# Rows of a Fourier stage's first batch: loaded from SBUF in four transfers a quad instead of by way of DRAM

## The chip, the cores and the metric

One Trainium2 chip, one core of it. The metric is device time in microseconds (us) of one execution of the whole program. The kernel before has a median of 1192.6 us in 3 runs (1191.81 to 1194.62).

## What is computed

Two batches of 3008 tokens with 256 features go through a Fourier layer and then through two feed-forward layers, all in float32:

```python
X = np.fft.rfft(x, axis=1)                       # x: (2, 3008, 256)
Yr = X.real @ w_r - X.imag @ w_i + b_r
Yi = X.real @ w_i + X.imag @ w_r + b_i
Y = shrink(Yr, 0.01) + 1j * shrink(Yi, 0.01)     # sign(v) * max(|v| - 0.01, 0)
x = np.fft.irfft(Y, n=3008, axis=1).reshape(6016, 256)
h = x @ moe_w_in                                 # 256 -> 2048
x = (h * clip(h + 3, 0, 6) / 6) @ moe_w_out      # 2048 -> 256
g = x @ moe2_w_gate                              # 256 -> 1536
out = (g * sigmoid(g) * (x @ moe2_w_val)) @ moe2_w_out
```

## The kernel before

The Fourier transform of length 3008 = 47 x 64 is done in two stages of matrix products. The first stage (`pre`, L315, products at L328 and L330) gives, for a batch, 96 rows of 32 x 256 numbers: 24 values of g, two parts and two halves of the real tokens, 32 values of j. A row is 8192 numbers, 32 KB. The first batch's rows lie in one SBUF tile, `first`, one row per partition; those of the second batch lie in `second` and in pieces of a ring.

The second stage (`s2`, L390, products at L397) wants these rows in another shape: for each g, the 4 rows that belong to it and the 32 values of j have to lie on 128 partitions with 256 numbers each. It works on a *quad* of four g at a time, six quads a batch, and its operand is the tile `z`, 128 partitions x 4 x 256, 512 KB, in three buffers. Going from 16 rows on 16 partitions to 128 partitions is the work of DMAs, and in the kernel before all of them go through scratch tensors `Bd` in DRAM.

For the first batch the rows of quad Q are the partitions Q, Q + 6, Q + 12 and so on of `first`, 16 in all. Quad 0 is written to `Bd[0]` from POOL's queue in four column pieces while the first stage still runs (L337, released by `sent`). The quads 1 to 5 are written whole by `group` (L351, L353), from SP's queue, each right after the load of the z before it (`load_q`, L380, L386). So z1 is loaded when `Bd[1]` has landed, and so on. The second batch goes through `Bd[6]` (written at L339 and L357) and its z are loaded at L386 also.

The order is written out by hand in `seq`: the second stage of quad p + 1 (`S`) begins with `ahead`, which issues the table `m` (L373) and the tile z of quad p + 2, so a z is asked for about one quad before it is used. Between them stand the products with the layer's weights (`ln`, L428, products at L441 to L446), the first inverse stage (`ia`, L464, products at L471, table `n`, results sent to `Cd` by POOL) and steps of `conv1`, which loads pieces of the feed-forward weights into `st` (L165) and converts them. SP issues nearly all loads, in program order. The tile framework gives the transfers of SP and ACT eight semaphores, DMAHW0 to DMAHW7, in turn; a transfer that takes one waits until the transfer that had it before has landed.

After these stages, some 190 us into the run, come the feed-forward layers, where TensorE works without a break.

Of the kernel before, what the change touches and what calls it, by code (L numbers as in the profile page):

```python
# [9 lines left out]
F32 = mybir.dt.float32  # L10
# [10 lines left out]
SEQ, DIM, NB = 3008, 256, 2  # L21
N1, NG, NJ, K2 = 47, 24, 32, 64
QN, GW = 2 * N1, 4 * NG

QP = 96
NQ = NG // 4
# [59 lines left out]
def fourier_moe_kernel(ctx: ExitStack, tc: tile.TileContext, x, lin, bias, w1, w2, fwd1, inv2, fwd2,  # L86
                       inv1, out):
    nc = tc.nc
# [3 lines left out]

    ps = ctx.enter_context(tc.tile_pool(name="ps", bufs=1, space=PSUM))
    dram = ctx.enter_context(tc.tile_pool(name="scratch", bufs=1, space=DRAM))
    Bd = [dram.tile([16 if n < NQ else GW, NJ * DIM], F32, name=f"Bd{n}") for n in range(NQ + 1)]
    Cd = [dram.tile([GW, NJ * DIM], F32, name=f"Cd{b}") for b in range(NB)]
    Xd = dram.tile([128, 2, TOK], F32, name="Xd")
    Wd = [dram.tile([128, SLOT * 128], F32, name=f"Wd{f}") for f in range(KF2)]
# [213 lines left out]
    first = w1p.tile([128, NT * TC], F32, tag="w1_o", name="first", bufs=1)  # L312
# [33 lines left out]

    REFILL = {1: 6, 3: 7}
    SINCE = {3: 0, 5: 4, 6: 6, 7: 7}
    bd1 = Bd[NQ].rearrange("(q r) c -> r q c", q=NQ)

    def group(Q):  # L351
        if 0 < Q < NQ:
            nc.sync.dma_start(Bd[Q], first[Q:GW:NQ])  # L353

    def write_second(i):
        c = slice(2 * i * TC, 2 * (i + 1) * TC)
# [10 lines left out]
    bview = [t.rearrange("(g w) (j d) -> (w j) g d", w=4, j=NJ) for t in Bd]  # L367
    cview = [[t[48 * q : 48 * q + 48].rearrange("(g c) (j d) -> (c j) g d", c=2, j=NJ) for q in range(2)] for t in Cd]
    m_t, z_t, n_t, X, yp = {}, {}, {}, {}, {}
# [6 lines left out]
    def load_m(b, Q):  # L376
        if (b, Q) not in m_t:
            m_t[b, Q] = table("m", fwd2, Q, f"m{b}_{Q}", 3)

    def load_q(b, Q):  # L380
        if (b, Q) in z_t or Q >= NQ:
            return
        load_m(b, Q)
        z_t[b, Q] = ap_.tile([128, 4, DIM], F32, tag="z", name=f"z{b}_{Q}", bufs=3)
        src = bview[NQ][:, Q * 4 : Q * 4 + 4, :] if b else bview[Q]
        nc.sync.dma_start(z_t[b, Q], src)  # L386
        if b == 0:
            group(Q + 1)

    def s2(b, Q, dh):  # L390

# [93 lines left out]
    def ahead(p):  # L485
        if p < len(ORDER):
            load_q(*ORDER[p])
# [7 lines left out]
    def L(p):  # L495
        return [lambda h=h: ln(*ORDER[p], h) for h in range(2)]

    def A(p):
        return [lambda: ia(*ORDER[p])] if p >= 0 else []

    P = [lambda n=n: pre(n) for n in range(NB * NT)]
    seq = [prepare] + P[:NT] + [lambda: load_q(0, 0)] + P[NT : NT + 2] + [lambda: load_q(0, 1)]
    seq += P[NT + 2 : NT + 5] + S(0) + P[NT + 5 : NT + 6]
    rest = P[NT + 6 :]
    for p in range(len(ORDER)):
        l, a = L(p), A(p - 1)
# [722 lines left out]
```

## Time and profile before

| | us |
|---|---|
| median of 3 runs | 1192.6 (1191.81 to 1194.62) |
| the profiled execution | 1195.22 |
| its span, first to last instruction | 1193.4 |
| TensorE (PE) busy | 1181.4 |
| VectorE (DVE) busy | 917.5 |
| ScalarE (ACT) busy | 775.5 |
| GpSimd (POOL) busy | 58.4 |
| mean granted TensorE clock | 0.999 of 2.4 GHz |

All times in a profile are from the start of the span. PE is the matmul side of TensorE and PEld its weight load, which overlaps it; SPq is SyncE's queue of DMA issues, and what stands behind an issue is the time that SP took to issue it, not that of the transfer. A transfer's own time is given apart, from issue to landing. L386 is line 386 of the kernel before; the code that loads z and the lines behind it stand two to four lines earlier in the changed kernel. A share of the DMA engines is the time that packets took, divided by that of 16 engines; packets of a stretch are counted by their start.

### The profile page before, as it was taken

What the parts mean: (1) busy time and instruction counts of PE and PEld (TensorE: products, weight loads), DVE (VectorE), ACT (ScalarE), POOL (GpSimd) and SP (SyncE); (2) the same over time, 40 slices, a digit from 0 to 9 for tenths busy, and PEclk for the clock granted to TensorE, in tenths of its full rate; (3) what the DMA queues carried; (4) which work ended last, traced back from release to release, by engine and by line L of the source; (5) the groups of instructions that cost most, each with busy time, mean ns of one, the idle gap of its engine ahead of it and who ended that gap; (6) DMA issues with size and microseconds to landing.
All of it is one profiled execution on the core that took longest, in us unless ns stands there. A gap on an engine that the chain in (4) does not pass through costs nothing.

```text
span 1193.4 us, 17934 instructions
## 1 busy us (share of the span) xinstructions
PE 1181.4 (99%) x6576; PEld 979.7 (82%) x6576; DVE 917.5 (77%) x1630; ACT 775.5 (65%) x1431; POOL 58.4 (5%) x91
## 2 busy tenths in 40 slices
PE   9999999999999999999999999999999999999998
PEld 3888887878888888888889888888888888888997
DVE  5678985898999989989888666766766766766665
ACT  3667765677777777777777655655655655655554
POOL 4011004500000000000000000000000000000000
PEclk9999999999999999999999999999999999999999
DMA  8898534964472563553543544644644644644552
GB/s 300 296 286 248 169 90 126 310 214 161 130 242 102 189 224 138 176 182 141 203 163 119 185 159 159 230 159 159 229 159 159 229 159 159 225 159 159 199 193 72
DMA packets 69208, 219.63 MB, mean 184 GB/s; under 512 B 6672, under 2 KB 29200, under 8 KB 57296
## 3 DMA queue, kind: packets, MB, share of 16 engines
q1 hardware_dynamic: 66144, 209.28, 51.2%
q0 software_dynamic: 2688, 9.05, 2.7%
q8 instruction: 51, 0.84, 0.3%
q14 instruction: 37, 0.30, 0.1%
q10 hardware_dynamic: 288, 0.16, 0.0%
HBM read 172.07 MB, written 46.40 MB: 183 GB/s over the span
## 4 chain that ended last, share of the span: by engine, by line
PE 90%; DMA 4%; DVE 3%; ACT 1%; issue 1%; POOL 1%; SPq 0%; DVEq 0%; ACTq 0%; POOLq 0%
PE acc L127 12%; PE acc L129 12%; PE acc L128 11%; PE P L931 8%; PE P L933 8%; PE P L932 8%; PE Tb L931 4%; PE Tb L933 4%; PE Tb L932 4%; PE Q L931 2%; PE Q L933 2%; PE Q L932 2%; PE p L471 2%; PE p L397 2%; DMA z<-Bd 1%; PE p L330 1%
## 5 line engine op out<-in xcount | busy, mean ns | idle before, releaser
L987 ACT COPY hold<-P 128x512 f32<-128x512 f32 (+1 forms) x224 | 128.3, 573 | 74.9 <-PE P L933 74.9
L613 ACT CAST gated<-r 128x512 fp32r<-128x512 f32 (+1 forms) x160 | 98.2, 614 | 58.4 <-DVE r L978 58.3
L132 DVE TENSOR_TENSOR gated<-s,gated 128x512 fp32r<-128x512 f32 (+1 forms) x144 | 97.4, 676 | 49.7 <-ACT gated L1114 49.5
L127 PE MATMUL acc<-gated,w_o 128*128 128x512 f32 (+1 forms) x320 | 124.1, 388 | 0.0
L132 DVE TENSOR_TENSOR gated<-r,gated 128x512 fp32r<-128x512 f32 (+1 forms) x160 | 107.8, 674 | 21.1 <-ACT gated L613 17.2
L982 DVE TENSOR_TENSOR hold<-Q,hold 128x512 f32<-128x512 f32 (+1 forms) x112 | 75.9, 678 | 62.4 <-PE Q L933 52.9
L128 PE MATMUL acc<-gated,w_o 128*128 128x512 f32 (+1 forms) x320 | 123.3, 385 | 0.0
L129 PE MATMUL acc<-gated,w_o 128*128 128x512 f32 (+1 forms) x320 | 123.2, 385 | 0.0
L974 ACT ACTIVATE r<-hold,consts 128x512 f32<-128x512 f32 (+1 forms) x120 | 85.7, 714 | 43.3 <-DVE hold L982 40.2
L129 PE MATMUL acc<-gated,slot 128*128 128x512 f32 (+1 forms) x288 | 111.1, 386 | 0.0
L127 PE MATMUL acc<-gated,slot 128*128 128x512 f32 (+1 forms) x288 | 111.0, 385 | 0.1
L128 PE MATMUL acc<-gated,slot 128*128 128x512 f32 (+1 forms) x288 | 110.9, 385 | 0.0
L982 DVE TENSOR_TENSOR hold<-P,hold 128x512 f32<-128x512 f32 (+1 forms) x112 | 75.8, 677 | 38.9 <-PE P L933 38.9
L1154 ACT ACTIVATE s<-hold 128x512 f32<-128x512 f32 (+1 forms) x72 | 44.8, 623 | 85.6 <-DVE hold L982 85.6
L931 PE MATMUL P<-xo,slot 128*128 128x512 f32 (+1 forms) x240 | 92.5, 385 | 2.8 <-DVE hold L982 2.7
L982 DVE TENSOR_TENSOR hold<-Tb,hold 128x512 f32<-128x512 f32 (+1 forms) x112 | 75.9, 678 | 24.8 <-PE Tb L933 18.2
L978 DVE SCALAR_TENSOR_TENSOR r<-r,hold 128x512 f32<-128x512 f32 (+1 forms) x120 | 81.2, 677 | 14.3 <-ACT r L974 13.2
L932 PE MATMUL P<-xo,slot 128*128 128x512 f32 (+1 forms) x240 | 91.6, 382 | 0.0
L933 PE MATMUL P<-xo,slot 128*128 128x512 f32 (+1 forms) x240 | 91.6, 382 | 0.0
L1114 ACT CAST gated<-s 128x512 fp32r<-128x512 f32 (+1 forms) x144 | 88.1, 612 | 2.2 <-DVE s L1169 2.2
L1159 ACT ACTIVATE s<-hold 128x512 f32<-128x512 f32 (+1 forms) x72 | 45.0, 625 | 50.8 <-DVE hold L982 50.8
L987 ACT COPY hold<-Tb 128x512 f32<-128x512 f32 (+1 forms) x112 | 64.9, 580 | 7.0 <-PE Tb L933 0.4
(190 smaller groups left out, 2869.8 us busy)
## 6 DMA issues: line engine op xcount, KB each, us to landing
slot<-Wd SPq DMA_DIRECT2D x72, 1152.0 KB, 5.1
slot<-Sd SPq DMA_DIRECT2D x40, 896.0 KB, 4.9
st<-in_w SPq DMA_DIRECT2D x68, 256.0 KB, 5.1
Wd<-slot SPq DMA_DIRECT2D x12, 1152.0 KB, 5.2
z<-Bd SPq DMA_DIRECT2D x12, 512.0 KB, 6.8
Cd<-cs POOLq DMA_DIRECT2D x24, 256.0 KB, 5.2
Xd<-x SPq DMA_DIRECT2D x20, 256.0 KB, 3.1
raw<-Xd SPq DMA_DIRECT2D x5, 1024.0 KB, 7.8
```

The lines of the kernel that those rows point to most:

```text
L127: nc.tensor.matmul(o, wl, xh, start=start, stop=False)
L128: nc.tensor.matmul(o, wh, xh, start=False, stop=False)
L129: nc.tensor.matmul(o, wh, xl, start=False, stop=stop)
L132: nc.vector.tensor_tensor(out=o, in0=full, in1=hi.bitcast(F32), op=ALU.subtract)
L613: nc.scalar.copy(hi[:, :n], g[:, :n])
L931: nc.tensor.matmul(o, wl, x[m][:, 0, :n], start=start, stop=False, skip_group_check=not start)
L932: nc.tensor.matmul(o, wh, x[m][:, 1, :n], start=False, stop=False, skip_group_check=not start)
L933: nc.tensor.matmul(o, wh, x[m][:, 0, :n], start=False, stop=True, skip_group_check=not start)
L974: nc.scalar.activation(r[:, :n], x[:, :n], AF.Relu, bias=three)
L982: nc.vector.tensor_tensor(out=h, in0=x[:, :n], in1=c, op=ALU.add)
L987: nc.scalar.copy(c, x[:, :n])
L1114: nc.scalar.copy(hi[:, :nb], t[:, :nb])
```

## The change

`Bd` shrinks to one tensor of 16 rows for quad 0 and one of 96 rows for the second batch. `group` and its five stores are gone. For quads 1 to 5 of the first batch `load_q` issues four transfers instead of one, each of which reads four rows of `first` and writes one of the four parts of z, 128 KB. Quad 0 and the second batch stay as they were.

```diff
-    Bd = [dram.tile([16 if n < NQ else GW, NJ * DIM], F32, name=f"Bd{n}") for n in range(NQ + 1)]
+    Bd = [dram.tile([GW if b else GW // NQ, NJ * DIM], F32, name=f"Bd{b}") for b in range(NB)]
...
-    bd1 = Bd[NQ].rearrange("(q r) c -> r q c", q=NQ)
-
-    def group(Q):
-        if 0 < Q < NQ:
-            nc.sync.dma_start(Bd[Q], first[Q:GW:NQ])
+    bd1 = Bd[1].rearrange("(q r) c -> r q c", q=NQ)
...
         z_t[b, Q] = ap_.tile([128, 4, DIM], F32, tag="z", name=f"z{b}_{Q}", bufs=3)
-        src = bview[NQ][:, Q * 4 : Q * 4 + 4, :] if b else bview[Q]
-        nc.sync.dma_start(z_t[b, Q], src)
-        if b == 0:
-            group(Q + 1)
+        if b or not Q:
+            nc.sync.dma_start(z_t[b, Q], bview[b][:, Q * 4 : Q * 4 + 4, :])
+            return
+        for g in range(4):
+            a = Q + 4 * NQ * g
+            nc.sync.dma_start(z_t[b, Q][:, g], first[a : a + 4 * NQ : NQ].rearrange("w (j d) -> w j d", j=NJ))
```

SP's queue before, from the load of z0 on. A name's number is the quad (`z_1` is z of quad 1) and then that of its buffer; what stands in brackets are the semaphores that the instruction waits for:

```order
L386 DMA z_0_238<-Bd_60 128x4x256 [waits DMASW5_49,DMASW4_49,DMAHW5_49,DMASW3_49,DMASW2_49]
L353 DMA Bd_61<-first 16x8192 [waits DMAHW6_49,DVE_49,Activation_49]
L373 DMA m_1_258<-in_fwd 128x512 [waits DMAHW7_49]
L386 DMA z_1_260<-Bd_61 128x4x256 [waits DMAHW6_49,DMAHW0_49]
L353 DMA Bd_62<-first 16x8192 [waits DMAHW1_49]
L373 DMA n_0_317<-in_inv 128x512 [waits DMAHW2_49]
L373 DMA m_2_346<-in_fwd 128x512 [waits DMAHW3_49]
L386 DMA z_2_348<-Bd_62 128x4x256 [waits DMAHW1_49,DMAHW4_49,DMASW0_49,DVE_49]
L353 DMA Bd_63<-first 16x8192 [waits DMAHW5_49]
```

The same place in the changed kernel:

```order
L382 DMA z_0_233<-Bd_60 128x4x256 [waits DMASW5_49,DMASW4_49,DMAHW5_49,DMASW3_49,DMASW2_49]
L369 DMA m_1_252<-in_fwd 128x512 [waits DMAHW6_49]
L386 DMA z_1_254<-first 128x1x256 [waits DMAHW7_49,DVE_49,Activation_49]
L386 DMA z_1_254<-first 128x1x256 [waits DMAHW0_49]
L386 DMA z_1_254<-first 128x1x256 [waits DMAHW1_49]
L386 DMA z_1_254<-first 128x1x256 [waits DMAHW2_49]
L369 DMA n_0_313<-in_inv 128x512 [waits DMAHW3_49]
L369 DMA m_2_342<-in_fwd 128x512 [waits DMAHW4_49]
L386 DMA z_2_344<-first 128x1x256 [waits DMAHW5_49,DMASW0_49,DVE_49]
L386 DMA z_2_344<-first 128x1x256 [waits DMAHW6_49]
L386 DMA z_2_344<-first 128x1x256 [waits DMAHW7_49]
L386 DMA z_2_344<-first 128x1x256 [waits DMAHW0_49]
```

The stores and the waits for them (DMAHW6 before z1, DMAHW1 before z2) are gone, z has four entries a quad, and the third of z2 (DMAHW7) now follows the landing of the first of z1. The order on the other engines is the same.

## Rows read from the trace of the kernel before

**Rows 1.** The page: part 1, and part 4, the chain by engine.

```profile
PE 1181.4 (99%) x6576; PEld 979.7 (82%) x6576; DVE 917.5 (77%) x1630; ACT 775.5 (65%) x1431; POOL 58.4 (5%) x91
...
PE 90%; DMA 4%; DVE 3%; ACT 1%; issue 1%; POOL 1%; SPq 0%; DVEq 0%; ACTq 0%; POOLq 0%
```

**Rows 2.** TensorE's waits, whole run: us in total, times, longest us.

```profile
PE p L397 <- DMA z<-Bd: 1.8, 1, 1.8
```

**Rows 3.** Timeline of PE: start us, us, instruction; in brackets idle time before it.

```profile
35.56 2.05 PE L397 MATMUL p<-m,z 128*128 128x128 f32 x16
...
63.04 1.95 PE L397 MATMUL p<-m,z 128*128 128x128 f32 x16
64.92 2.00 PE L471 MATMUL p<-yp,n 64*128 64x256 f32 x16
...
73.73 2.62 PE L397 MATMUL p<-m,z 128*128 128x128 f32 x16 [1.84 <-DMA z<-Bd]
76.28 3.02 PE L471 MATMUL p<-yp,n 64*128 64x256 f32 x16
```

**Rows 4.** Chain that ended last, in order of time: start us, us, what.

```profile
30.52 5.00 DMA z<-Bd
...
62.08 11.52 DMA z<-Bd
```

**Rows 5.** Busy time by stretch; behind POOL's: granted clock, DMA share, GB/s.

```profile
73.70:80.00 6.30, 6.27 (x37) 5.30 (x38) 3.11 (x7) 3.27 (x8) 0.00 (x0) 0.73 0.67 209
```

**Rows 6.** Timeline of SP's queue: start us, us of issuing, transfer.

```profile
24.95 0.40 SPq L386 DMA_DIRECT2D z<-Bd  x1
25.46 0.57 SPq L353 DMA_DIRECT2D Bd<-first  x1
...
30.52 0.38 SPq L386 DMA_DIRECT2D z<-Bd  x1
```

**Rows 7.** Waits of SP's queue: us in total, times, longest us.

```profile
SPq L386 <- DMA Bd<-first: 17.6, 5, 7.6
```

**Rows 8.** Transfers issued from 24 to 26 us: count, KB each, us to landing.

```profile
z<-Bd SPq DMA_DIRECT2D x1, 512.0 KB, 4.0
Bd<-first SPq DMA_DIRECT2D x1, 512.0 KB, 5.0
```

**Rows 9.** DMA from 25 to 72 us by queue: packets, MB, share of 16 engines.

```profile
q1 hardware_dynamic: 5597, 10.84, 68.9%
q0 software_dynamic: 771, 2.63, 19.2%
```

**Rows 10.** Instructions on `first`: ns of issuing, min/median/max, first and last start.

```profile
L353 SPq DMA_DIRECT2D Bd<-first x5: 512/689/2194, 25.5 to 51.0; - x5
```

**Rows 11.** Instructions on `z` from 20 to 75 us, the same columns.

```profile
L386 SPq DMA_DIRECT2D z<-Bd x6: 377/380/4103, 25.0 to 62.1; - x6
```

**Rows 12.** DMA packets from 25.7 to 28.7 us, and q1's share.

```profile
DMA packets 542, 1.02 MB, mean 339 GB/s; under 512 B 15, under 2 KB 527, under 8 KB 527
...
q1 hardware_dynamic: 542, 1.02, 102.1%
```

**Rows 13.** The same from 26.2 to 27.8 us, z0's load alone.

```profile
DMA packets 320, 0.33 MB, mean 205 GB/s; under 512 B 0, under 2 KB 320, under 8 KB 320
...
q1 hardware_dynamic: 320, 0.33, 68.9%
```

**Rows 14.** The same from 132.9 to 134.4 us, a z of the second batch.

```profile
DMA packets 339, 0.33 MB, mean 221 GB/s; under 512 B 15, under 2 KB 339, under 8 KB 339
...
q1 hardware_dynamic: 339, 0.33, 63.1%
```

**Rows 15.** The same from 101.3 to 102.1 us, the load of ct.

```profile
DMA packets 16, 0.18 MB, mean 225 GB/s; under 512 B 0, under 2 KB 0, under 8 KB 0
...
q1 hardware_dynamic: 16, 0.18, 127.9%
```

## The prediction

> **What bounds the kernel now.** I read the page first. TensorE is busy for 99% of the span and makes 90% of the chain that ended last, DMA 4% of it [rows 1]. So the change can pay only where TensorE stands still for a z tile, and it costs wherever it makes one later. The list of TensorE's waits has one such entry in the whole run: 1.8 us, once, at L397 for a z read from Bd [rows 2]. The timeline gives the place: the second-stage products of quad 5 start at 73.73 us after 1.84 us of standing still, and those of quad 1 at 35.56, just behind the landing of z1, issued at 30.52 and 5.00 us on its way, with nothing to spare [rows 3, 4]. The stall has a tail. Quad 5's products took 2.62 us where quad 4's took 1.95, and the inverse products behind them 3.02 against 2.00 [rows 3]: in that stretch the granted clock is 0.73, that is, part of it at 1.2 GHz instead of 2.4 [rows 5]. The tail is (2.62 - 1.95) + (3.02 - 2.00) = 1.7 us, so all that waiting for z costs today is 1.84 + 1.7 = 3.5 us.
>
> Then SP's timeline: load z0 at 24.95, store group 1 at 25.46, load z1 only at 30.52 [rows 6]. SP stood 17.6 us in five waits for those stores to land [rows 7]. Undisturbed, z lands 4.0 us after its issue and a store in 5.0 [rows 8]; z5, issued at 62.08, took 11.5 [rows 4]. From 25 to 72 us the 16 DMA engines are 68.9 + 19.2 = 88.1% busy [rows 9]. This stretch has little DMA time to give away.
>
> **The change, part by part.** *Removed:* five stores of 512 KB, SP's 17.6 us of waiting for them and 2.5 MB of reads from DRAM. On SP the five stores (median 689 ns, [rows 10]) and five loads (380 ns, [rows 11]) give way to 20 loads of about 380 ns: 20 x 0.38 = 7.6 us for 5 x (0.69 + 0.38) = 5.4. SP is on no path there and the 17.6 us of waits go, so I cost these 2.2 us at nothing; were that cover gone, each later quad's z would be some 0.5 us later. Behind a blocked z load stand m, n and the piece of w1 that the conversion needs, all used about a quad later. The order also shows that a transfer waits for the one eight places ahead of it: the third part of z2 waits for the first part of z1. SP may still run about a quad ahead, as far as the three z buffers allow.
>
> *Added:* the same 512 KB per quad, in four transfers that each read four rows of `first`. How they spread over the 16 engines decides. In the stretch with z0 and the first store, the packets over 8 KB are 15, with (1.02 - 0.52) MB between them: one is one 32 KB row [rows 12]. So a store of 16 rows is 16 pieces for 16 engines. Every other transfer of the stretch has 16, 64, 96 or 128 rows on each side; none has four (the code tells it), so the trace doesn't show how four are dealt. I take it that a row goes to one engine as it does in the store: four rows, four engines, and, with nothing in the rows that speaks for rotating, the same four for every part. [...]
>
> The destination rows are 1 KB, so each of the four engines moves 4 x 32 = 128 pieces of 1 KB per quad instead of z's 32 pieces and one 32 KB row. Price of a piece: between 26.2 and 27.8 us only z0 moves, 320 pieces at a share of 0.689: 0.689 x 16 x 1.6 / 320 = 55 ns [rows 13]. Low end: 0.631 x 16 x 1.5 / 324 = 47 ns in a calmer stretch (339 packets less 15 of a few bytes, [rows 14]). High end: the ct load into 48 rows, 16 pieces of 11 KB, 1.279 x 16 x 0.8 / 16 = 1.02 us each, 93 ns per KB [rows 15]. I take 55: same piece, same tile, same stretch. Price of a 32 KB row: (1.021 x 16 x 3.0 - 512 x 0.055) / 15 = 1.39 us [rows 12].
>
> *The sum, for one of the four engines, 25 to 72 us:* busy 0.881 x 47 = 41.4 us, idle 5.6. Off: five z's, 5 x 32 x 0.055 = 8.8, and five rows, 6.9. On: 5 x 128 x 0.055 = 35.2. Net +19.5; the idle 5.6 swallows a part, +13.9. The other traffic left, 41.4 - 15.7 = 25.7 us, loses its competitors for DRAM; at 47 for 55 ns it shrinks by 15%, 3.8 us. So z5 lands 10 to 14 us later, I say 12. TensorE waits for it; the tail at 1.2 GHz stays as it is; behind z5, z of the second batch shifts along, and from there TensorE is the bound and gives nothing back. Waits will not all stand at quad 5: z1 is due at 35.5 and four engines need 7 us for it behind z0, so a stall of about 1 us begins there and grows by 2 to 4 per quad.
>
> At 47 ns: 5 x 128 x 0.047 = 30.1, less 15.7, 5.6 and 3.8, gives +5. At 93: 59.5 - 15.7 - 5.6 = +38. The profiled execution is 1195.2 us (span 1193.4); it would become 1207. It stands 2.6 over the median of 1192.6, so on the median: 1192.6 + 12 = **1204.6 us**.
>
> **Rivals.**
> *A, the parts spread over all engines* (or over different fours). Then every engine has 8.8 + 6.9 - 8.8 = 6.9 us less to do, SP issues z earlier by its lost waits, z5 is there before 71.9, and stall and tail go: 1192.6 - 3.5 = 1189.1. For it: nothing in the trace has four rows, so nothing forbids it. Against: a row has been one engine's piece in the store. It decides if the wait at L397 vanishes. Chance 0.19.
> *B, the four engines also get in each other's way in z's rows.* In the ct load pieces cost 93 ns per KB on 48 rows against 55 on 128 [rows 13, 15], so few rows written at once are dearer. Then +20 to +38, 1213 to 1231. Against: z has 128 rows, and four engines ask for less than sixteen. [...] Chance 0.20.
> *C, four engines, but hidden:* SP runs ahead by what it waited before, and the other traffic shrinks by more than 15%, so that z5 is as late as now. The low price with 3 us more relief does it: 1192.6. For it: a 32 KB row, which is 1.39 us, is 43 ns per KB. Chance 0.12.
>
> **How the numbers follow.** The forecast (+4 to +20) has 0.49, A 0.19, B 0.20, C 0.12. About 0.2% (2.4 us) is what a measurement here can tell from no change. Faster is A, 0.19; within is C, 0.12; slower the rest, 0.69. The range reaches down to A with half a microsecond of margin, 1188.5, and up to 1224, which leaves out the upper half of B; with the forecast alone it would be 1197 to 1213.
>
> **What would show it.** Right: TensorE's waits hold an entry at L397 for z read from first, several times, 10 us or more in all; in the first 90 us the mean DMA share falls well under 0.88 while TensorE waits for DMA, the mark of a few loaded engines; the parts land in far more than 4.0 us; Bd<-first shrinks to POOL's four. Only the size wrong: the same picture with another price per piece. Wrong: no wait for z at L397, parts that land in 3 to 4 us, a granted clock of 1.00 around 74 us (A); or a single wait of about 2 us as now (C).

## The result and the profile after

The changed kernel takes 1200.34 us (median of 5 runs, 1198.56 to 1202.31), the kernel before, in runs beside it, 1192.07 (1191.40 to 1194.62). The ratio is 1.0066, 95% interval 1.0055 to 1.0076: slower by 8.3 us, where 12.5 were forecast from 1192.1 (1204.6, range 1188.5 to 1224). The profiled execution took 1199.77 us, its span is 1198.0.

TensorE's waits of the changed kernel, whole run (us in total, times, longest us):

```profile
PE p L395 <- DMA z<-first: 4.3, 5, 2.1
PE P L929 <- DVE hold L980: 2.6, 3, 1.3
```

The one wait for z of [rows 2] has become five, 4.3 us in all. The timeline of PE shows where they are:

```profile
29.85 1.95 PE L395 MATMUL p<-m,z 128*128 128x128 f32 x16
...
35.73 1.95 PE L395 MATMUL p<-m,z 128*128 128x128 f32 x16
...
45.16 1.38 PE L395 MATMUL p<-m,z 128*128 128x128 f32 x10 [0.32 <-DMA z<-first]
...
54.99 1.95 PE L395 MATMUL p<-m,z 128*128 128x128 f32 x16
...
63.68 2.13 PE L395 MATMUL p<-m,z 128*128 128x128 f32 x16
65.74 2.00 PE L469 MATMUL p<-yp,n 64*128 64x256 f32 x16
...
73.23 0.46 PE L395 MATMUL p<-m,z 128*128 128x128 f32 x2 [0.52 <-DMA z<-first]
74.51 0.49 PE L395 MATMUL p<-m,z 128*128 128x128 f32 x2 [0.82 <-DMA z<-first]
77.12 0.80 PE L395 MATMUL p<-m,z 128*128 128x128 f32 x2 [2.12 <-DMA z<-first]
78.48 2.51 PE L395 MATMUL p<-m,z 128*128 128x128 f32 x10 [0.55 <-DMA z<-first]
80.91 2.81 PE L469 MATMUL p<-yp,n 64*128 64x256 f32 x16
```

Quads 1, 3 and 4 find their z there, and quad 2 waits 0.32 us. Quad 5 gets its four parts one by one, the last at 78.48, against 73.73 in [rows 3]: 0.52 + 0.82 + 2.12 + 0.55 = 4.0 us of waiting. The clock follows (busy time of each engine by stretch; behind POOL's: granted clock, DMA share, GB/s):

```profile
63.00:72.00 9.00, 9.00 (x73) 8.21 (x73) 7.11 (x16) 6.49 (x16) 1.28 (x2) 1.00 0.89 256
72.00:84.00 12.00, 7.99 (x40) 6.19 (x39) 5.48 (x12) 4.02 (x11) 0.00 (x0) 0.72 0.82 248
```

A clock of 0.72 over 12 us is 6.7 us at the lower level, which is 0.50 (that is the granted clock from 75.80 to 82.50 us; in the kernel before it is 0.50 from 75.00 to 78.30), and in part of them TensorE stood still. Measured as the prediction measured it, the tail is (0.46 + 0.49 + 0.80 + 2.51 - 1.95) + (2.81 - 2.00) = 3.1 us, where it was 1.7 in the kernel before; a part of it is not the clock but the cutting of sixteen products into four groups, since two products take 0.46 us by themselves.

Two views tell what the DMA engines did. First, the stretch of 29.0 to 31.1 us, in which nothing but parts of z1 moves (packets, then q1's share of 16 engines):

```profile
DMA packets 202, 0.20 MB, mean 97 GB/s; under 512 B 4, under 2 KB 202, under 8 KB 202
...
q1 hardware_dynamic: 202, 0.20, 27.2%
```

0.272 x 16 = 4.4 engines at work and 97 GB/s, with two parts of 128 KB and more in the queue. A piece costs 0.272 x 16 x 2.1 / 198 = 46 ns, where z0's load took 55 [rows 13]. Second, the packets of the whole run, on the page of the kernel before and on that of the changed one:

```profile
DMA packets 69208, 219.63 MB, mean 184 GB/s; under 512 B 6672, under 2 KB 29200, under 8 KB 57296
```

```profile
DMA packets 69048, 217.01 MB, mean 181 GB/s; under 512 B 6592, under 2 KB 29120, under 8 KB 57216
```

Gone are five stores and five loads with 16 + 512 pieces, and the small packets of these transfers, which I take for their completions, one per engine that takes part; under 512 B there are 80 fewer. A load of 128 rows has sixteen of them (e2 below counts 240 more for 15 loads more). At sixteen each the ten transfers had 160, so the 20 new ones post 80, four each; the stretch above, in which one part of z1 ends, holds four. SP's queue is no longer held by the stores of [rows 7], but by the issues of z's parts, most from quad 4 on (start us, us of issuing, transfer; then ns of one issue, min/median/max):

```profile
31.75 4.20 SPq L386 DMA_DIRECT2D z<-first  x4
...
48.69 8.35 SPq L386 DMA_DIRECT2D z<-first  x4
...
63.41 7.86 SPq L386 DMA_DIRECT2D z<-first  x4
...
L386 SPq DMA_DIRECT2D z<-first x20: 538/980/2712, 26.0 to 69.0; - x20
```

One issue takes 0.98 us in the median where the prediction had 0.38.

From 25 to 72 us the DMA engines are 48.0 + 21.2 = 69.2% busy (88.1% in [rows 9]):

```profile
q1 hardware_dynamic: 4944, 7.26, 48.0%
q0 software_dynamic: 804, 2.76, 21.2%
```

The DMA engines do less in all, and yet z5 comes later: that is the mark of a few loaded engines.

### The profile page after: what moved, and what is told of

It is laid out like the page before. It is cut to its first block, busy times and chain, and to the rows that moved or that the text cites. A ratio compares the mean times of both kernels' runs of the same rounds, so it can differ in the third digit from the quotient of the medians.

```text
span 1198.0 us, 17944 instructions
## 1 busy us (share of the span) xinstructions
PE 1182.5 (99%) x6576; PEld 980.6 (82%) x6576; DVE 917.4 (77%) x1630; ACT 776.7 (65%) x1431; POOL 58.5 (5%) x91
## 4 chain that ended last, share of the span: by engine, by line
PE 88%; DVE 5%; DMA 3%; ACT 2%; SPq 1%; issue 1%; POOL 0%; ACTq 0%; DVEq 0%; POOLq 0%
PE acc L127 11%; PE acc L129 11%; PE acc L128 11%; PE P L929 8%; PE P L931 8%; PE P L930 8%; PE Tb L931 4%; PE Tb L929 4%; PE Tb L930 4%; PE Q L931 2%; PE Q L929 2%; PE Q L930 2%; PE p L469 2%; PE p L330 2%; DMA z<-first 2%; PE p L395 2%
```

## The experiments

**Four rows against four parts.** Both kernels keep the way through DRAM, and both load each z in four transfers of 128 KB. In e1 a transfer has four rows, held apart by padding; in e2 it has 128.

```diff
# e1_dram_four_rows, quads 1 to 5 of the first batch; Bd[1] to Bd[5] are 256 numbers wider
-        nc.sync.dma_start(z_t[b, Q], src)
+        for g in range(4):
+            nc.sync.dma_start(z_t[b, Q][:, g], Bd[Q][4 * g : 4 * g + 4].rearrange("w (j d) -> w j d", j=NJ))
# e2_dram_four_parts
+            nc.sync.dma_start(z_t[b, Q][:, g], bview[Q][:, g])
```

> Three theories. T (mine): a transfer whose source has four rows uses four DMA engines, always the same four; they carry 128 pieces of 1 KB per quad and z5 comes late. I: it is the issuing, four transfers a quad instead of one on SP's queue and its eight semaphores. S: it is the source, pieces read out of four partitions of SBUF are slow. This kernel keeps the way through DRAM (stores included) and loads each of z1 to z5 in four transfers of four rows; the rows in DRAM are padded by 1 KB so that the four rows stay a dimension of their own. T: at 47 ns a piece the four engines carry 5 x (128 - 32) x 0.047 = 22.6 us more than in the kernel before, less 5.6 of idle time: z5 10 to 17 us later, 1200 to 1210, and 12 completion packets fewer for each such transfer than a full one has. I: as the changed kernel, about 1200. S: no SBUF source, 1190 to 1194.

> Way through DRAM as before, each of z1 to z5 loaded in four transfers of 128 rows x 1 KB on each side (128 rows each, no dimension of four). T: 16 engines as before, SP has 15 issues more (about 6 us) beside other work: 1190 to 1195. I: about 1200, since the queue and the semaphores are used as in the changed kernel and the stores come on top. S: 1190 to 1195.

Measured: e1 1208.30 us (ratio 1.0126, 1.0099 to 1.0153), e2 1196.59 (1.0031, 1.0010 to 1.0051), before 1193.04. The source is DRAM in both and the number of issues is the same; the rows alone make 11.7 us. The pages count 6672 packets under 512 B in e1, as many as before, and 6912 in e2: the 20 transfers post 80 completions in e1, four each, and 320 in e2, sixteen each. Stretches in which only z's pieces start show the same, 35.2 to 36.1 us of e1 and then 40.2 to 41.4 of e2:

```profile
DMA packets 87, 0.09 MB, mean 98 GB/s; under 512 B 1, under 2 KB 87, under 8 KB 87
...
q1 hardware_dynamic: 87, 0.09, 27.5%
```

```profile
DMA packets 381, 0.35 MB, mean 289 GB/s; under 512 B 42, under 2 KB 381, under 8 KB 381
...
q1 hardware_dynamic: 381, 0.35, 94.6%
```

z's pieces keep 4.4 engines busy and move at 98 GB/s, against 15 engines and 289 GB/s. The other engines are not idle in e1's stretch: a view that begins half a microsecond earlier has twelve packets of over 8 KB, rows of a store that are still under way.

```profile
DMA packets 145, 0.52 MB, mean 375 GB/s; under 512 B 5, under 2 KB 133, under 8 KB 133
```

A piece costs 0.275 x 16 x 0.9 / 86 = 46 ns in e1, as in the changed kernel, though the source here is DRAM. That is T, and it ends S: four rows are slow without an SBUF source, and with one the piece is no dearer. It is not the length of an issue either: in e1 an issue takes 0.53 us in the median, less than in the changed kernel, and the loss is larger. But e2 is not free. Its 1196.59 us lie above T's 1190 to 1195, 3.5 us over the kernel before; four transfers a quad in place of one cost something of their own, and no run shows by which way.

**Another queue, and one row at a time.** e3 issues the 20 transfers from POOL, e4 cuts each into four of one row, whose 32 pieces T deals to 16 engines, which nothing had shown before this run.

```diff
# e3_direct_pool
-            nc.sync.dma_start(z_t[b, Q][:, g], first[a : a + 4 * NQ : NQ].rearrange("w (j d) -> w j d", j=NJ))
+            nc.gpsimd.dma_start(z_t[b, Q][:, g], first[a : a + 4 * NQ : NQ].rearrange("w (j d) -> w j d", j=NJ))
# e4_direct_one_row
+            for w in range(4):
+                r = a + NQ * w
+                nc.sync.dma_start(z_t[b, Q][32 * w : 32 * w + 32, g], first[r : r + 1].rearrange("w (j d) -> w j d", j=NJ))
```

> The changed kernel with the 20 four-row transfers issued from POOL's queue instead of SP's. [...] I: SP has 20 issues fewer, 1188 to 1193. S: source unchanged, about 1200 or more.

> The changed kernel with each four-row transfer cut into four of one row (32 pieces of 1 KB to 32 partitions, the slowest dimension that is not 1 is 32 on both sides), 16 a quad on SP's queue. T: such a transfer is dealt to 16 engines, two pieces each, so the load is even; SP issues 80 transfers of about 0.4 us, 6.4 us a quad of some 8.5, and eight in flight of 32 KB: 1189 to 1196. I: four times the issues of the changed kernel, 1205 to 1220. S: 1200 or more.

e3: 1202.02 us (1.0077, 1.0058 to 1.0097). I (1188 to 1193) missed; S (about 1200 or more) hit, and had been ruled out by e1. T had left two outcomes open: parts spread over all 16 engines, 1188 to 1193, which missed, and the same four engines as on SP's queue, 1199 or more, which hit. Yet the parts do not all use the same four engines here: between 24 and 26 us, when only POOL's queue moves, its share is 42.4%, 6.8 engines. Nor is z5 sent late: POOL issues it from 63.22 us on, SP in the changed kernel from 63.41. But it stands right behind two stores of Cd and one of the second batch in POOL's queue, and the DMA share from 63 to 72 us is 0.95. Issued from 60 to 72 us are (count, KB each, us to landing):

```profile
Bd<-second SPq DMA_DIRECT2D x1, 768.0 KB, 13.6
st<-in_w SPq DMA_DIRECT2D x2, 256.0 KB, 10.1
z<-first POOLq DMA_DIRECT2D x4, 128.0 KB, 15.7
```

These transfers take 10.1 to 15.7 us to land, and TensorE stands still for 5.44 us before quad 5. Whether the queue or the traffic made z5 late is not settled, so e3 decides nothing about T beyond those 6.8 engines.

e4: 1224.89 us (1.0276, 1.0253 to 1.0299). T had 1189 to 1196 and fell short by 29 us; I, with 1205 to 1220, by 5. T took 0.4 us for an issue. SP's queue shows the sixteen of quads 1 and 3:

```profile
25.88 11.58 SPq L388 DMA_DIRECT2D z<-first  x16
...
50.30 14.31 SPq L388 DMA_DIRECT2D z<-first  x16
```

That is 0.72 and 0.89 us each, waits included: a transfer waits for the one eight places ahead, as the order of the changed kernel has it. The load was spread, if each engine posts one completion (the page counts 70248 packets, 1040 more than before, which is 16 completions for each of the 80), but SP had become the bound: the five quads' issues fill 60 us, and TensorE waits 18.0 us for z. That is I's mechanism, at four times the issues of the changed kernel. The pieces were dearer, too. From 42 to 48 us only z's parts move:

```profile
DMA packets 457, 0.31 MB, mean 52 GB/s; under 512 B 153, under 2 KB 457, under 8 KB 457
...
q1 hardware_dynamic: 457, 0.31, 59.2%
```

That is 0.592 x 16 x 6 / 304 = 187 ns a piece, the small completions included, against 46 in the changed kernel.

**What can be gained at all.** e0 is the kernel before once more, e5 leaves the move out.

```diff
# e5_no_move, in load_q
+        if b == 0 and Q:
+            z_t[b, Q] = z_t[0, 0]
+            return
```

> The kernel before, unchanged, for a second profile of it: is the wait for z5 (1.84 us, and 1.7 us of half clock behind it) there in every execution? T: yes if the span is near 1193; an execution near 1190 should show it short or absent.

> The changed kernel without any move of quads 1 to 5: their products take the z of quad 0, and the 20 transfers are left out (so the first batch's second stage is computed from quad 0's rows). It bounds what any way of moving these rows can give: no wait for z1 to z5, DMA engines with 5.2 MB less to carry. T: 1187 to 1190, with no wait at L395 for z of the first batch. If it stays at 1192, the wait for z5 in the kernel before is not worth its 3.5 us in a median execution. I and S say the same.

e5: 1192.49 us (0.9998, 0.9989 to 1.0008): no gain. TensorE has no wait for z there, as expected, but 1187 to 1190 was missed. e0, one execution: 1192.93 us, span 1191.1. In this execution quad 5 doesn't wait; the waits for z are one of 1.34 us at quad 1 and one of 0.38 at quad 0, and the clock stays at 1.00:

```profile
37.05 2.05 PE L397 MATMUL p<-m,z 128*128 128x128 f32 x16 [1.34 <-DMA z<-Bd]
...
73.22 1.95 PE L397 MATMUL p<-m,z 128*128 128x128 f32 x16
```

The 3.5 us read from [rows 3] are those of one execution, 1195.2, which lies 3 us above the median. There was nothing to win here, however the parts are spread over the engines.

**How many quads direct.** The kernel before, with only some quads direct (four transfers of four rows out of `first`) and the rest through DRAM.

```diff
# e6: DIRECT = (5,)   e7: (3, 5)   e9: (1, 3, 5)   e10: (2, 3, 4, 5)
+        if 0 < Q < NQ and Q not in DIRECT:
             nc.sync.dma_start(Bd[Q], first[Q:GW:NQ])
```

> The kernel before with quad 5 alone direct (four four-row transfers from SBUF), quads 1 to 4 through DRAM. T: one direct quad adds 128 x 0.047 - 32 x 0.047 - 1.39 = +3.1 us to the four engines, less than their idle time of 5.6, and takes 2.9 from the twelve others: no later than before, 1189 to 1194. I: a fifth of the changed kernel's loss, 1193 to 1195. S: z5 is the one that is waited for, so a slow source shows whole: 1195 to 1200.

> As the one before with quads 3 and 5 direct. T: +6.2 us on the four engines, against 5.6 of idle time and some relief on what else they carry: break-even, 1190 to 1195. I: two fifths of the loss, 1195 to 1197. S: as quad 5 alone, 1195 to 1200.

> The kernel before with quads 1, 3 and 5 direct, 2 and 4 through DRAM. T: a direct quad adds 3.1 us to the four engines; 5.6 of idle time and some 3.8 of relief are free, so three quads (9.3) are about where the loss begins: 1192 to 1195. I (every direct quad costs the same, 8.2 / 5 = 1.6): 1197.

> The kernel before with quads 2 to 5 direct, 1 through DRAM. T: 12.4 on the four engines less 9.4: +3, 1195 to 1198. I: 4 x 1.6, 1198.7.

| direct quads | us | ratio, 95% interval |
|---|---|---|
| 5 | 1192.78 | 1.0008, 0.9996 to 1.0019 |
| 3, 5 | 1193.92 | 1.0018, 1.0004 to 1.0032 |
| 1, 3, 5 | 1192.32 | 0.9998, 0.9988 to 1.0009 |
| 2, 3, 4, 5 | 1199.18 | 1.0057, 1.0037 to 1.0076 |
| 1 to 5 (the change) | 1200.34 | 1.0066, 1.0055 to 1.0076 |

Three direct quads cost nothing, four cost nearly all; two (3, 5) came out at 1.8 us, just clear of noise, so the series is not even. I's price per quad, the same for each, hit e10 (1198.7) but missed e7 and e9 (1195 to 1197, and 1197) and is out. A queue that overflows fits. TensorE's waits in e10's profiled execution say so too; all four stand at quad 5:

```profile
PE p L403 <- DMA z<-first: 5.2, 4, 2.4
```

In e9's there is no wait for z from first. T hit e6, e7 and e9, and its budget missed e10 by 1 us. It counts quads, and it may matter whether a quad through DRAM lies between two direct ones: four in a row leave the four engines no quad in which to catch up. That reading of e9 against e10 fits both numbers, but no run kept the count and changed the order alone.

**Taking work from the four engines.** e8 is the changed kernel with the first store of the second batch moved behind z5.

```diff
-        if p in (2, 3):
-            seq += [lambda i=p - 2: write_second(i)]
+        if p == 3:
+            seq += [lambda i=i: write_second(i) for i in range(2)]
```

> The changed kernel with both stores of the second batch (768 KB each) issued after z5's four transfers instead of one before and one after. Nothing is taken from SP's issues or from z5's own transfers, only one store of 48 KB per engine from the queue ahead of z5. T: the four engines are behind with their queue, so z5 comes 48 KB x 0.043 = 2.1 us earlier; what the first quad of the second batch then waits for (two stores in a row behind z5) may give a part of it back: 1197 to 1200, and the wait at L395 for z of first shorter by about 2 us. I: the order of the issues ahead of z5 changes by one of many, no change of z5, 1199 to 1201.

Measured: 1198.37 us (1.0052, 1.0031 to 1.0073), 2.0 under the changed kernel's median; the two intervals overlap, so the time alone decides nothing. The waits point T's way, in one profiled execution of each kernel (us in total, times, longest us):

```profile
PE p L395 <- DMA z<-Bd: 4.1, 1, 4.1
...
PE p L395 <- DMA z<-first: 2.6, 2, 2.4
```

The wait for z from first falls from 4.3 to 2.6 us, 1.7 less for the 2.1 forecast, and z5's last part is used at 75.01 instead of 78.48. The first quad of the second batch then waits 4.1 us for the two stores, as was feared: what one transfer is spared, the next ones pay.

## Why the prediction was right, and where not

- *Four rows, four engines:* shown, by the 27.2% in the changed kernel, by four completions a transfer, and by e1 against e2. No row of the kernel before shows how four rows are dealt; that a row goes to one engine was carried over from the store's 32 KB rows [rows 12]. It held for four rows (4.4 engines, four completions) and not for one row of 32 pieces, which posts 16 completions in e4; what decides the number is not shown. That it is always the same four engines is inferred, since nothing in the profile numbers them: from 29.0 to 31.1 us two parts and more are in the queue, and with a different four for each part more than 4.4 engines would have been at work.
- *The price of a piece* is the term that was mis-sized. I took 55 ns from z0's row; it was 46, the low end. With 47 the sum put z5 5 us later (6.3, had it repriced the five loads that go, 7.5 us for 8.8), and it came 78.48 - 73.73 = 4.75 us later. The 55 was not competition with other transfers, since z0 moves alone in [rows 13]. Packet by packet that trace has a median of 46 ns, and a few pieces of up to 392 ns make the mean; what held those up is not shown.
- *Why then 8.3 us and not 5:* the sum took the wait at quad 5 and its tail for part of every execution and subtracted only a constant 2.6 between the profiled one and the median. A typical execution (e0) has neither. Against e0 the changed kernel's profile has 4.3 us of waits and 3.1 of tail, less e0's 1.7: +5.7, where the spans differ by 1198.0 - 1191.1 = 6.9. I had also left the tail as it was; it nearly doubled. Two omissions made up for a part of a price that was too high, so that 1204.6 came within 4.3 us of the result is in part luck.
- *SP's 2.2 us at nothing:* 20 issues were put at 7.6 us. A quad's four took 3.35 to 8.35 us, 27.4 in all, and e2 paid 3.5 us for four transfers a quad. In the changed kernel this part cannot be told from the rest; in e9, with 12 such issues, it doesn't show.
- *Waits from quad 1 on, growing, 10 us or more in all:* wrong, it was 4.3 us. The loads, freed of the stores, came in time for quads 1, 3 and 4, quad 2 waited 0.32 us, and only quad 5, with a store of the second batch ahead of it, was late in earnest.
- *Rival A* would not have given 1189.1: even with no move at all it is 1192.5. *B* is out in this kernel, at 46 ns a piece. *C* is what e9 shows, three direct quads that stay hidden; five don't (and C's own sum, the low price with 3 us more relief, leaves +2 and not 0).

## What to carry to other kernels

Before a transfer is made more direct, look at how many rows it has on each side, and count the engines of one like it in a calm stretch: here four rows read kept 4.4 engines busy and 128 rows 15. The bytes saved in DRAM did not pay with four engines out of sixteen carrying the rest: the mean DMA share from 25 to 72 us fell from 88.1 to 69.2%, and z5 came 4.75 us later. Read a piece's price from a calm stretch as well as a busy one, and ask which of the two the changed kernel will be. And before a wait is counted as a gain, see in a second profile or without the work altogether whether it is there in the median.

## What had not been expected of the hardware

One row of 32 KB written to 32 partitions posts 16 completions (e4), while four such rows in one transfer post four (the changed kernel), which I read as sixteen engines and four. But one row in a transfer costs 187 ns a piece in engine time, where four rows cost 46; whether that comes from the one partition that is read or the 32 that are written, no run tells.

The length of a wait alone did not decide whether the clock fell. In e8 TensorE stood still for 2.35 us at quad 5, and the granted clock from 72 to 84 us is 1.00; in e7 it stood still for 2.73 us before the second batch, and the clock is 1.00 from 72 to 96 us. In the kernel before 1.84 us at quad 5 were followed by a clock of 0.73 [rows 5]. Behind e8's 4.13 us before the second batch it fell as well (the products, then the stretch, granted clock behind POOL's):

```profile
87.42 3.56 PE L395 MATMUL p<-m,z 128*128 128x128 f32 x16 [4.13 <-DMA z<-Bd]
...
84.00:92.00 8.00, 4.58 (x26) 4.40 (x28) 2.88 (x8) 2.44 (x6) 0.00 (x0) 0.79 1.04 378
```

The runs don't settle what makes the difference.
